# Storing paired-order output tiles with one transfer each in a fused retention and mixer kernel

## The chip, the cores and the metric

The kernel runs on one core of one Trainium2 chip. The metric is device time in microseconds (us) of one execution, the median of several runs. A run over 1.5% above the fastest of its kernel is called slow; ratios compare fast runs with fast runs. A profiled run adds a trace; the span of a profile is a little different from the timed median. Engines are named as follows: PE is TensorE's matmuls, PEld its weight loads, DVE is VectorE, ACT is ScalarE, POOL is GpSimd, SP is SyncE. A "q" after SP or ACT means the instruction queue of that engine, from which transfers are issued.

## The reference

```python
def reference(q, k, v, moe_U, moe_V, moe_w_ch1, moe_w_ch2):   # cut
    # q, k, v: (4, 8, 768, 64) float32: batch, heads, tokens, head dim
    state = 0
    for t in range(768):                      # retention, per head, decay gamma_h
        state = gamma * state + outer(k[:, :, t], v[:, :, t])
        y[:, :, t] = q[:, :, t] @ state / 8
    x = y as (4, 768, 512)
    u  = x + (x^T @ U @ V)^T                  # mixes the 768 tokens, rank 32
    return u + relu(u @ w_ch1) @ w_ch2        # 512 -> 2048 -> 512
```

The output is (4, 768, 512) float32: four batches of six tiles of 128 tokens, 256 KB a tile.

## The kernel before

The kernel works on the batches in a pipeline: while TensorE computes the MLP (`relu(u @ w_ch1) @ w_ch2`) of one batch, the retention of the next one is woven in. Tokens are held in pairs. Of a block of 128 tokens, partition 0 to 63 hold the even tokens and 64 to 127 the odd ones. So partition `64*two + p` is token `2*p + two`, and an output tile must be taken apart when it is stored:

```python
    HP = P // 2                       # 64
    stores = []

    def store():
        if stores:
            eng, dst, src = stores.pop(0)
            dst = dst.rearrange("(p two) c -> two p c", two=2)
            for i in range(2):
                eng.dma_start(out=dst[i], in_=src[ds(HP * i, HP)])
```

Each tile is two transfers of 64 partitions; each writes every second row of the block, in rows of 2 KB. Who issues them depends on the batch (batches count from 0):

```python
            # batch 0, after each tile's last sum:
                    stores.append((nc.scalar if b else nc.sync,
                                   out[b, ts(j, P)], o_sb))
            # batches 1 to 3:
            if end and i + 1 == NP:                    # last tiles of batch 3: half a tile
                stores.append((nc.sync, out[b, ts(j, P), ds(DQ * h, DQ)],
                               r[0][:, ds(DQ * h, DQ)]))
            elif r[1] == 2:
                stores.append((nc.sync if b > 1 else nc.scalar,
                               out[b, ts(j, P)], r[0]))
            # ... batch 3's last two tiles have more such pieces (quarters)
```

Batch 0's stores are kept until the end of its MLP (`weave(b == 1, ...)` keeps them) and then leave SyncE's queue all together. Batch 1's leave ScalarE's queue; those of batches 2 and 3 leave SyncE's as they are ready. SyncE's queue also carries every load and three kinds of DMA transposes, which read SBUF and write SBUF: `kT` and `qT` for the retention, and `uT`, the transposed input of the MLP, three for each of batches 2 and 3 (batches 0 and 1 get theirs in another way):

```python
    def lr_turn(b, j):                         # uT of two blocks of 128 tokens
        nc.sync.dma_start_transpose(
            out=uTs[b][:, ds(j, 2)].rearrange("p j c t -> p (j c) t"),
            in_=us[b][:, ds(j, 2)].rearrange("p j m -> p (j m)"))
```

The first two uT of a batch serve the first 512 tokens of its up-projection, and the third serves the other 256. The up-projection can't start without the first two, and not go past the eighth group of matmuls without the third.

## Time and profile before

| | before |
|---|---|
| median, at first | 226.73 us (3 runs, 225.97 to 227.8) |
| TensorE busy, of the 228.1 us span | 216.0 us (95%) |
| TensorE's longest wait | 1.8 us |
| store issues | 54 (40 from SP, 14 from ACT) |
| packets | 84,921 |

The head of the profile page (busy us, share of the span, number of instructions), and its DMA lines; each digit of the DMA line is the busy share, in tenths, of the 16 DMA engines in one fortieth of the span:

```profile
PE 216.0 (95%) x2235; PEld 148.4 (65%) x2235; DVE 140.8 (62%) x294; ACT 89.3 (39%) x187; POOL 91.8 (40%) x129
...
DMA  6997899999999999988999999000001990000263
...
DMA packets 84921, 38.83 MB, mean 170 GB/s; under 512 B 58816, under 2 KB 77984, under 8 KB 84896
```

TensorE is the bottleneck and is nearly always busy, so a transfer costs time only where TensorE waits for it, or at the very end. The waits view of TensorE (who waited for whom: total us, times, longest us) shows how little that is:

```profile
PE mlp L757 <- ACT gT L764: 1.8, 1, 1.8
...
PE mlp L757 <- DMA uT<-x: 0.5, 1, 0.5
```

The issue list of the page gives the stores' size and the median time from issue to landing:

```profile
out_dram<-o SPq DMA_DIRECT2D x32, 128.0 KB, 2.4
out_dram<-o ACTq DMA_DIRECT2D x12, 128.0 KB, 4.0
out_dram<-o SPq DMA_DIRECT2D x6, 64.0 KB, 2.1
```

The timeline of SyncE's queue (start us, us, engine and line, operation, times) shows where stores stand among other transfers:

```profile
94.87 7.59 SPq L608 DMA_DIRECT2D out_dram<-o  x12
102.51 1.33 SPq L155 DMA_DIRECT2D in<-in_k_dram  x2
...
174.44 3.71 SPq L608 DMA_DIRECT2D out_dram<-o  x6
178.32 3.87 SPq L591 DMA_TRANSPOSE uT<-x  x2
...
214.27 11.41 SPq L608 DMA_DIRECT2D out_dram<-o  x16
```

At 94.87 us batch 0's twelve halves go out just ahead of batch 3's 18 loads. At 174.44 batch 2's stand ahead of batch 3's uT transposes. From 214.27 to the end at 228.1 is the tail. Batch 1's stores leave ScalarE's queue between 123 and 138 us.

The stretches view (busy us of PE, PEld, DVE, ACT, POOL, then TensorE's granted clock, busy share of the DMA engines, GB/s) of batch 0's stores and of the tail:

```profile
97.50:105.50 8.00, 7.26 (x73) 4.42 (x71) 7.96 (x16) 4.70 (x12) 1.24 (x1) 1.00 0.91 205
...
214.30:228.10 13.80, 9.12 (x100) 8.20 (x97) 4.99 (x13) 0.00 (x0) 0.00 (x0) 0.91 0.49 114
```

Six tiles take 8 us at about 205 GB/s with the DMA engines nearly all busy (0.91). (The records of their packets run from 96.1 to 103.9 us; from 96 to 104 us the view reads 202 GB/s.)

### The profile page before, as it was taken

How to read it: one execution, taken by the hardware profiler on the slowest of the kernel's cores; microseconds unless marked ns; L12 is line 12 of the kernel's file. 1: busy time of each engine (PE TensorE's matmuls, PEld its weight loads, DVE VectorE, ACT ScalarE, POOL GpSimd, SP SyncE). 2: the span in 40 equal slices, each digit the busy share in tenths (PEclk: the TensorE clock that was granted, in tenths of full speed). 3: DMA queues.
4: the chain of work that ended last, by engine and by line, in shares of the span. 5: the costliest groups of instructions: out<-in, count | busy, mean ns of one | idle time of the engine just before them, and what ended most of it. 6: DMA issues, size and time to landing. Idle time of an engine off the chain costs nothing.

```text
span 228.1 us, 5543 instructions
## 1 busy us (share of the span) xinstructions
PE 216.0 (95%) x2235; PEld 148.4 (65%) x2235; DVE 140.8 (62%) x294; ACT 89.3 (39%) x187; POOL 91.8 (40%) x129
## 2 busy tenths in 40 slices
PE   7988999999899999989999996999999999999991
PEld 3677844595455454756887852656888846668891
DVE  6488556325274473899896653497868443857551
ACT  3256654474555126576411005567410035550000
POOL 5456777985879698930499400000000000000000
PEclk9999999999999999999999997999999999999997
DMA  6997899999999999988999999000001990000263
GB/s 177 299 290 211 239 367 288 367 357 228 239 181 240 242 228 180 192 205 210 237 236 229 215 252 193 1 0 3 0 3 42 154 204 17 3 1 0 48 148 83
DMA packets 84921, 38.83 MB, mean 170 GB/s; under 512 B 58816, under 2 KB 77984, under 8 KB 84896
## 3 DMA queue, kind: packets, MB, share of 16 engines
q1 hardware_dynamic: 83776, 36.84, 70.4%
q10 hardware_dynamic: 1120, 1.64, 2.4%
q8 instruction: 17, 0.28, 0.6%
q14 instruction: 8, 0.07, 0.1%
HBM read 27.46 MB, written 6.29 MB: 148 GB/s over the span
## 4 chain that ended last, share of the span: by engine, by line
PE 57%; DMA 17%; SPq 9%; DVE 8%; issue 3%; POOL 3%; ACT 1%; ACTq 0%; POOLq 0%; DVEq 0%
PE mlp L757 24%; PE A L649 9%; PE mlp L805 7%; DMA in<-in_moe_w_ch_dram 6%; SPq L155 5%; DMA in<-in_k_dram 4%; PE C L649 3%; DMA in<-in_q_dram 3%; SPq L591 3%; PE B L649 2%; DVE gS L599 2%; DMA qT<-qd 2%; PE s L505 2%; DVE a L511 2%; PE o L527 2%
## 5 line engine op out<-in xcount | busy, mean ns | idle before, releaser
L757 PE MATMUL mlp<-uT,w1b 128*128 128x512 f16 (+1 forms) x512 | 90.6, 330 | 2.5 <-ACT gT L764 1.8
L757 PEld LDWEIGHTS <-w1b 128*128 128x128 f16 x512 | 48.8, 99 | 34.9 <-issue 5.4
L764 ACT ACTIVATE gT<-mlp 128x512 f16<-128x512 f32 (+1 forms) x94 | 45.2, 491 | 66.0 <-PE mlp L757 30.8
L762 DVE TENSOR_SCALAR gT<-mlp 128x512 f16<-128x512 f32 (+1 forms) x34 | 18.9, 555 | 32.2 <-PE mlp L757 32.2
L511 DVE TENSOR_TENSOR a<-s,mask 128x512 bf16<-128x512 f32 x36 | 23.1, 682 | 12.6 <-PE s L505 12.4
L649 PEld LDWEIGHTS <-gT 128*128 128x128 f16 x288 | 27.5, 98 | 3.5
L805 PE MATMUL mlp<-w2b,gT 128*128 128x512 f16 x96 | 24.1, 380 | 0.0
L306 POOL TENSOR_TENSOR kd<-in,gk 128x512 bf16<-128x512 f32 x18 | 19.3, 1084 | 5.5 <-DMA in<-in_k_dram 5.5
L649 PEld LDWEIGHTS <-gS 128*128 128x128 f16 x200 | 19.3, 98 | 2.6
L85 ACT ACTIVATE x<-o 128x512 f16<-128x512 f32 x20 | 11.9, 595 | 21.5 <-PE o L527 21.3
L306 POOL TENSOR_TENSOR qd<-in,gq 128x512 bf16<-128x512 f32 x18 | 19.1, 1078 | 1.0 <-DMA in<-in_q_dram 1.0
L649 PE MATMUL A<-w2t,gT 128*128 128x256 f16 x144 | 18.3, 273 | 0.0
L85 ACT ACTIVATE state<-st 64x256 bf16<-64x256 f32 x40 | 15.0, 375 | 6.0 <-PE st L385 4.1
L805 PEld LDWEIGHTS <-gT 128*128 128x128 f16 x96 | 8.2, 98 | 7.5
L304 POOL CAST vd<-in 128x512 bf16<-128x512 f32 x18 | 11.2, 628 | 2.7 <-DMA in<-in_v_dram 2.2
L342 POOL CAST w1b<-in 128x512 f16<-128x512 f32 x16 | 9.7, 616 | 3.1 <-DMA in<-in_moe_w_ch_dram 2.7
L348 POOL CAST w2b<-in 128x512 f16<-128x512 f32 x16 | 9.7, 616 | 0.9 <-DMA in<-in_moe_w_ch_dram 0.2
L564 DVE TENSOR_TENSOR x<-s,x 128x256 f16<-128x256 f32 (+1 forms) x16 | 8.1, 550 | 2.1 <-ACT gT L764 1.1
L649 PE MATMUL B<-w2b,gT 128*128 128x256 f16 x72 | 9.4, 273 | 0.0
L649 PE MATMUL A<-w2t,gS 128*128 128x256 f16 x72 | 9.2, 273 | 0.0
L649 PE MATMUL A<-w2b,gT 128*128 128x256 f16 x72 | 9.0, 273 | 0.0
L527 PE MATMUL o<-vd,a 128*128 128x64 bf16 x144 | 7.7, 193 | 0.8 <-DVE a L511 0.8
(148 smaller groups left out, 278.4 us busy)
## 6 DMA issues: line engine op xcount, KB each, us to landing
in<-in_moe_w_ch_dram SPq DMA_DIRECT2D x32, 256.0 KB, 5.4
in<-in_k_dram SPq DMA_DIRECT2D x24, 256.0 KB, 5.3
in<-in_q_dram SPq DMA_DIRECT2D x24, 256.0 KB, 5.0
in<-in_v_dram SPq DMA_DIRECT2D x24, 256.0 KB, 5.4
out_dram<-o SPq DMA_DIRECT2D x32, 128.0 KB, 2.4
out_dram<-o ACTq DMA_DIRECT2D x12, 128.0 KB, 4.0
out_dram<-o SPq DMA_DIRECT2D x6, 64.0 KB, 2.1
Uf<-in_moe_U_dram SPq DMA_DIRECT2D x1, 96.0 KB, 5.8
```

The source lines that it names most:

```text
L85: nc.scalar.activation(dst, src, AF.Copy)
L155: nc.sync.dma_start(out=t, in_=src)
L304: nc.gpsimd.tensor_copy(out=t, in_=src)
L306: nc.gpsimd.tensor_tensor(t, src, g, op=ALU.mult)
L342: nc.gpsimd.tensor_copy(out=w1b[:, c, ts(mb, 512)], in_=take("w1", mb, c))
L511: nc.vector.tensor_tensor(a, four(sp[i]), causal(mask), op=ALU.mult)
L527: nc.tensor.matmul(o_p[:, ts(h, D)], a[i][:, h // 2], vb[:, h], start=(ci == 0 and h == 0), stop=True, skip_group_check=True)
L649: nc.tensor.matmul(acc[key, i], lhs[:, m, ts(i, P)], rhs[:, m], start=(fresh and m == 0), stop=(m == NH - 1), skip_group_check=True)
L757: nc.tensor.matmul(g_p[:, :sz], w1b[:, c, ts(m, P)], uTs[b][:, ds(j, nj), c], start=(c == 0), stop=(c == NCB - 1))
L762: nc.vector.tensor_relu(gT[:, m, ds(lo, sz)], g_p[:, :sz])
L764: nc.scalar.activation(gT[:, m, ds(lo, sz)], g_p[:, :sz], AF.Relu)
L805: nc.tensor.matmul(ch, gT[:, m, ts(j, P)], w2b[:, m], start=(m == 0), stop=(m == NM - 1))
```

## The change

The intent is half as many store issues, with transfers twice as large: the whole tile of 128 partitions goes in one transfer, and the pairs are taken apart by the access pattern of the DRAM side.

```diff
     def store():
         if stores:
             eng, dst, src = stores.pop(0)
-            dst = dst.rearrange("(p two) c -> two p c", two=2)
-            for i in range(2):
-                eng.dma_start(out=dst[i], in_=src[ds(HP * i, HP)])
+            eng.dma_start(out=dst.rearrange("(p two) c -> two p c", two=2),
+                          in_=src)
```

The SBUF side is 128 rows of 512 elements. The DRAM side is now a pattern of 2 x 64 x 512. Each row is still 2 KB, and the same bytes go to the same places. (Line numbers fall by one: a matmul of L757 before is L756 after.)

## The prediction

> **What bounds the kernel now.** TensorE is busy 216.0 of the 228.1 us span (the page's busy line) and holds 57% of the chain of waits; the waits view shows no TensorE wait over 1.8 us after 84 us. Stores matter in three places (the timeline). (a) From 95 us batch 0's six tiles leave SyncE's queue, just ahead of batch 3's 18 loads. (b) From 123 to 138 us batch 1's tiles leave ScalarE's queue, beside the transposes for batches 2 and 3. (c) From 174 us batch 2's tiles share SyncE's queue with batch 3's uT transposes (the chain shows uT 2.5 + 3.2 us, up to 184.1). Then the tail: first batch-3 store issued at 214.3, last at 225.1, end 228.1.
>
> **What the change removes.** 54 store issues become 27, each about 0.56 us of a queue: 15 us of issue, perhaps 1 us of it on the chain. Bytes and data packets (2 KB rows) stay.
>
> **What it adds.** The DRAM side becomes a 2 x 64 x 512 pattern, outermost dimension 2, not 64. [...] A 2 KB packet that met no traffic took 84 ns in the trace; 64 on one engine are 5.4 us for a 256 KB tile, about 7.4 us from issue to landing, against 2.4 us now. All tiles queue on the same two engines: six take 32 us (before: 8 us, 97 to 105 us).
>
> **Where that meets the critical path.** The program gives transfers eight completion semaphores in turn, so an issue also waits for the transfer eight before it, on either queue.
> 1. Batch 3's loads stand behind the stores on two engines: first landing about 132 instead of 107 us, last about 151. ScalarE's first batch-1 store waits for the 13th load (about 146), its last for an earlier store; ScalarE can't evacuate until 162 to 175 instead of 138. Batch 2's up-projection starts 24 to 36 us later, perhaps with a further stall for its third uT: estimate +33 us.
> 2. Batch 3's uT transposes stand behind three stores, then three more: +12 us to its start, +12 us before its second half: +24 us.
> 3. Tail: 1.5 MB through two engines is about 34 us (2 KB at 84, 1 KB at 45, 512 B at 27 ns); with latency 37 us after the first store instead of 13.8: +23 us.
>
> Sum: 226.7 + 33 + 24 + 23 = 307 us; I shade it to 303 us, range 262 to 332. Chances: faster by over 2% 0.04, within 2% 0.05, slower by over 2% 0.91.
>
> **What would show it.** The span to 95 us unchanged. Packets fall by about 810 (27 x 2 completion packets for 54 x 16), to some 84,110. Median store landing over 10 us. About 48 GB/s and 2/16 DMA share at the end, TensorE idle. TensorE waits near 138 and 184 us plus shifts. If stores still use 16 engines: packets fall by only 432, landings stay near 3 us, and time is within 1%.
>
> **What would make it wrong.** Engines chosen by the SBUF side's 128 (then same); loads overtaking stores; arbitration between the two queues kinder or harsher than packet by packet, which sizes step 1; a two-engine store faster than 84 ns per row.

## The result and the profile after

| | before | after |
|---|---|---|
| median of 4 runs | 226.75 us (225.97 to 227.8) | 318.1 us (317.39 to 318.59) |
| ratio of fast runs | | 1.402 (95% interval 1.396 to 1.409) |
| span of the profile | 228.1 us | 316.4 us |

A ratio is the mean time of one kernel's fast runs over that of the other's of the same rounds, so it is not quite the ratio of the medians. The change makes the kernel 40% slower, and the result is correct.

The head of the page and its DMA lines, after:

```profile
PE 220.5 (70%) x2235; PEld 150.4 (48%) x2235; DVE 140.7 (44%) x294; ACT 89.5 (28%) x187; POOL 91.1 (29%) x129
...
DMA  7999999999991122999999980000192910001111
...
DMA packets 84111, 38.82 MB, mean 123 GB/s; under 512 B 58006, under 2 KB 77174, under 8 KB 84086
```

The work is the same (DVE, ACT and POOL are busy as long as before), but the span grew by 88.3 us. Two things point at the cause. The packet count fell by exactly 810. In the trace of before a plain transfer ends with 16 packets of 4 bytes (called completion packets here); the nine stores of the tail after end with 2 each. 54 stores of 16 replaced by 27 stores of 2 is 864 - 54 = 810, and the 4-byte packets of the traces fell by just that, from 3,137 to 2,327. And the DMA line reads 1, about two sixteenths (a share of 0.12), at the end, where only stores run.

The waits view of TensorE, and the store lines of the tile view (duration of the issue in ns, min/median/max; first and last start):

```profile
PE mlp L756 <- DMA uT<-x: 66.5, 4, 34.0
...
L606 SPq DMA_DIRECT2D out_dram<-o x20: 512/2888/6394, 92.4 to 305.3; - x20
L606 ACTq DMA_DIRECT2D out_dram<-o x7: 522/533/4937, 140.4 to 290.2; - x7
```

TensorE waited 66.5 us for uT, against 0.5 before. Issuing a store held SyncE's queue for 2.9 us in the median and up to 6.4, against 0.57 (median) before. The issue list of this page has no landing times, for stores or loads, so the predicted landing can't be read there:

```profile
out_dram<-o SPq DMA_DIRECT2D x16, 256.0 KB
```

The timeline of SyncE's queue:

```profile
92.45 20.08 SPq L606 DMA_DIRECT2D out_dram<-o  x6
112.58 10.64 SPq L155 DMA_DIRECT2D in<-in_k_dram  x2
...
218.70 4.80 SPq L606 DMA_DIRECT2D out_dram<-o  x3
223.68 13.17 SPq L591 DMA_TRANSPOSE uT<-x  x2
...
281.08 27.57 SPq L606 DMA_DIRECT2D out_dram<-o  x8
```

The stretches of batch 0's stores, of a long wait of TensorE, of the first us after a wait, and of the tail:

```profile
95.00:127.00 32.00, 31.82 (x366) 24.70 (x365) 26.67 (x56) 11.72 (x26) 1.06 (x2) 1.00 0.20 66
146.00:162.00 16.00, 0.00 (x0) 0.00 (x0) 0.00 (x0) 0.00 (x0) 0.61 (x1) 0.50 0.96 77
187.20:192.50 5.30, 5.28 (x36) 3.70 (x37) 1.97 (x6) 1.70 (x5) 0.00 (x0) 0.62 0.00 0
...
281.10:316.40 35.30, 9.14 (x100) 8.22 (x97) 4.99 (x13) 0.00 (x0) 0.00 (x0) 0.68 0.12 45
```

Batch 0's six tiles now take 32 us instead of 8, while TensorE is still busy. In the tail the DMA engines are at a share of 0.12, that is 2 of 16, and move 45 GB/s. TensorE ends its work in the first 9 us of it and the stores go on for 26 more. From 146 to 162 us TensorE does nothing, at a granted clock of 0.50, while the DMA engines are nearly all busy (0.96) and yet move only 77 GB/s; an experiment below comes back to that.

Three marks of the timelines of SyncE's queue divide the loss. They are the first store of batch 0, of batch 2 and of batch 3:

| stretch | before | after | longer by | predicted |
|---|---|---|---|---|
| start to first batch-0 store | 94.87 | 92.45 | -2.4 | 0 |
| to first batch-2 store | 79.57 | 126.25 | 46.7 | 33 |
| to first batch-3 store | 39.83 | 62.38 | 22.6 | 24 |
| to the end | 13.8 | 35.3 | 21.5 | 23 |
| sum (spans) | 228.1 | 316.4 | 88.3 | 80 |

Most of the third line (19.6 of 22.6 us) is two waits of TensorE, for the uT pair of batch 3 and for its third uT, in the changed kernel's timeline (in brackets: idle time before it, and what ended it):

```profile
238.91 8.81 PE L756 MATMUL mlp<-uT,w1b 128*128 128x512 f16 x32 [11.09 <-DMA uT<-x]
256.18 4.08 PE L756 MATMUL mlp<-uT,w1b 128*128 128x256 f16 x21 [8.46 <-DMA uT<-x]
```

The first line is the scatter of single runs: in the other profiles, in which nothing differs up to this mark, it lies between 90.7 and 95.2 us.

### The profile page after: what moved, and what is told of

Its sections match the earlier page's. It is cut to its first block, busy times and chain, and to the rows that moved or that the text cites. A ratio compares the mean times of both kernels' runs of the same rounds, so it can differ in the third digit from the quotient of the medians.

```text
span 316.4 us, 5507 instructions
## 1 busy us (share of the span) xinstructions
PE 220.5 (70%) x2235; PEld 150.4 (48%) x2235; DVE 140.7 (44%) x294; ACT 89.5 (28%) x187; POOL 91.1 (29%) x129
## 2 busy tenths in 40 slices
DMA packets 84111, 38.82 MB, mean 123 GB/s; under 512 B 58006, under 2 KB 77174, under 8 KB 84086
## 4 chain that ended last, share of the span: by engine, by line
PE 40%; DMA 25%; SPq 17%; DVE 5%; POOL 2%; issue 2%; ACT 1%; POOLq 0%; DVEq 0%
PE mlp L756 15%; DMA uT<-x 10%; SPq L155 7%; PE A L648 6%; DMA in<-in_v_dram 6%; SPq L591 5%; DMA in<-in_moe_w_ch_dram 5%; PE mlp L804 5%; SPq L474 4%; DMA in<-in_k_dram 4%; PE C L648 2%; PE mlp L189 2%; PE B L648 2%; DVE gS L599 1%; PE s L505 1%
## 5 line engine op out<-in xcount | busy, mean ns | idle before, releaser
L756 PE MATMUL mlp<-uT,w1b 128*128 128x512 f16 (+1 forms) x512 | 95.4, 342 | 66.6 <-DMA uT<-x 66.5
L756 PEld LDWEIGHTS <-w1b 128*128 128x128 f16 x512 | 50.6, 102 | 102.0 <-DMA uT<-x 67.5
L87 DVE COPY qO<-qT 128x512 bf16<-128x512 bf16 x12 | 3.9, 366 | 30.4 <-DMA qT<-qd 30.4
```

What stands on the lines that cost most here:

```text
L756: nc.tensor.matmul(g_p[:, :sz], w1b[:, c, ts(m, P)], uTs[b][:, ds(j, nj), c], start=(c == 0), stop=(c == NCB - 1))
```

## The experiments

The theory: the outermost dimension of the DRAM side, 2, puts each store on two DMA engines (2 completion packets a store, a DMA share of 0.12 in the tail). All stores then form one line on these two, by estimate 5.4 us a tile (64 rows of 84 ns). Loads and transposes, it assumes, have a share on each of 16 engines, the two among them (a load ends with 16 completion packets in the trace, which names no engine), so they wait for that line too; and TensorE waits for the transposes.

Rival 1: fewer issues shift the turn of the eight completion semaphores (101 and 103 to 109 in the traces, one an issue), and so the waits. Rival 2: a strided store from all 128 partitions is slow in itself. Rival 3, which the prediction itself held for a part of the loss: ScalarE is held by its own stores and can't evacuate for TensorE.

The kernels of the first table below give wrong rows on purpose.

### More rows in the outermost dimension: 16, 8 and 4

```diff
-            eng.dma_start(out=dst.rearrange("(p two) c -> two p c", two=2),
+            eng.dma_start(out=dst.rearrange("(p n) c -> n p c", n=16),   # 8, 4
                           in_=src)
```

One transfer a tile, the same bytes in rows of 2 KB, the same issues and semaphores; only the outermost dimension (and which row goes where, wrongly) differs from the changed kernel.

> The changed kernel with 16 in place of 2 as the outermost dimension of the DRAM pattern (rows go to the wrong places on purpose; one transfer a tile, the same rows of 2 KB, the same issues and semaphores). Theory (the outermost dimension sets how many engines carry a store): sixteen engines, 84,111 + 27 x 14 = 84,489 packets, store landing near 3 us, 225 to 229 us. Rival 1 (fewer issues shift the turn of the eight semaphores and so the waits): about 318 us, since issues and semaphores are those of the changed kernel. Rival 2 (a strided store from all 128 partitions is slow in itself): about 318 us.

> As n16 with 8 (wrong rows on purpose). Theory: eight engines, a tile takes 16 x 84 ns = 1.3 us on each, six tiles about 8 us as the halves of before; packets 84,273; 225 to 233 us. Rivals 1 and 2: about 318 us.

> As n16 with 4 (wrong rows on purpose). Theory: four engines, a tile takes 32 x 84 ns = 2.7 us on each, six tiles 16 us; packets 84,165; tail +6, batch 3's uT +6, loads and batch 1's stores +8: 238 to 255 us. Rivals 1 and 2: about 318 us.

| outermost dimension | median us | before, same job | ratio of fast runs | packets | 2 KB rows per us, batch 0's stores |
|---|---|---|---|---|---|
| 2 (the change) | 318.1 | 226.75 | 1.402 | 84,111 | 23.9 |
| 4 | 264.57 (4 runs) | 227.89 | 1.170 (1.154 to 1.187) | 84,165 | 42.7 |
| 8 | 236.65 (4 runs, 1 fast: 231.62) | 227.89 | none given | 84,273 | 67.7 |
| 16 | 224.25 (6 runs) | 227.89 | 0.994 (0.984 to 1.005) | 84,489 | 119.6 |
| 64 twice (before) | | | | 84,921 | 98.1 |

The last column counts the records of 2 KB packets in the traces, from the first to the last of batch 0's. All four packet counts are exactly those of n completion packets a store. With 16 the whole loss is gone, though issues, semaphores, row size and the 128 partitions are those of the changed kernel. So rivals 1 and 2 fall. (Seven of the eleven runs before in this job are slow; the median of the four fast ones is 225.8 us, and the ratios use these. The record classes 4 as "unclear", as it does two runs below, though all three intervals lie above 1.1; the reason isn't on record.)

The dose fits in direction, but the rate doesn't grow in step with n: with 8 the six tiles took 11.3 us instead of the 8 expected. The size with 4 was expected too small (238 to 255, measured 264.57): TensorE waited 29.6 us for uT in that run, the same kind of wait that the prediction undersized. With 8 only one run counts as fast (231.62, inside the expected range); the others, 236 to 239 us, don't, and how much 8 costs is not settled.

The stretch of batch 0's stores with 16, to be read against the 205 GB/s of before (their packets run from 92.0 to 98.5 us, where the view reads 264):

```profile
93.30:99.70 6.40, 6.07 (x58) 3.78 (x58) 6.26 (x14) 4.02 (x9) 1.29 (x2) 1.00 1.02 270
```

The stores themselves do gain from one transfer of 128 partitions, when it ends with 16 completion packets: about 265 GB/s, in one profile of each kernel, with other rows written than before. In batch 0's stretch a 2 KB packet of a 64-partition half took 152 ns in the median (mean 142), one of these stores 84 ns (mean 117); why is not shown. The kernel's gain, 0.6%, is not clear of noise; the waits view of before shows no TensorE wait for stores that could be won.

### The change for some batches only

```diff
     def store():
         if stores:
-            eng, dst, src = stores.pop(0)
+            eng, dst, src, one = stores.pop(0)
+            if one:                       # b == 0, 1, 2, 3, or b < 2
+                eng.dma_start(out=dst.rearrange("(p two) c -> two p c", two=2),
+                              in_=src)
+                return
             dst = dst.rearrange("(p two) c -> two p c", two=2)
             ...
```

> The change for batches 0 and 1 only, the halves of before for batches 2 and 3 (right result). Theory: the first term alone; the first batch-2 store comes 44 to 48 us later than before, as in the changed kernel, and nothing is added after it: 226.7 + 46 = 270 to 277 us. The prediction had 33 us for this term (260). Rival: stages interact (the late stores need the early ones' backlog), so the sum of the parts falls well short of the whole: under 265 us here.

> The change for batch 0 only. Theory: batch 3's loads stand behind 32 us of stores on two engines, and ScalarE's first batch-1 store waits for the 13th of them; but batch 1's stores do not share the two engines row by row with the transposes: batch 2's up-projection starts 12 to 18 us later, no long second wait for uT: 237 to 247 us. If the queue sharing does not matter, this alone gives nearly all of the first term: about 270 us.

> The change for batch 1 only. Theory: 384 store rows a queue on two engines from about 124 us, turn by turn with the transposes' 256-byte packets (102 ns instead of 18 for one of them): batch 2's first uT pair about 12 us later and its third about 10 us more: 240 to 256 us. If the queues did not share the engines packet by packet: under 235 us.

> The change for batch 2 only. Theory: batch 3's uT transposes behind three stores, then three more: +20 to +24 us, 246 to 252 us; store rows before the transposes in the same queue, transposes' packets at 18 ns, not 102.

> The change for batch 3 only. Theory: the tail alone: first batch-3 store to the end about 35 us instead of 13.8: 246 to 250 us, everything before it unchanged within 2 us.

| changed batches | median us | before, same job | longer by | ratio of fast runs |
|---|---|---|---|---|
| 0 | 247.9 | 227.24 | 20.7 | 1.090 (1.082 to 1.099) |
| 1 | 252.2 | 227.24 | 25.0 | 1.113 (1.107 to 1.120) |
| 0 and 1 | 275.05 | 227.89 | 47.2 | 1.223 (1.211 to 1.234) |
| 2 | 252.13 | 227.24 | 24.9 | 1.112 (1.103 to 1.122) |
| 3 | 248.9 | 227.24 | 21.7 | 1.097 (1.091 to 1.103) |
| all | 318.1 | 226.75 | 91.4 | 1.402 |

All results are correct. The medians are of all runs, slow ones too. By medians of fast runs alone the differences are 19.7, 25.1, 49.2, 25.0, 21.8 and 91.4 us. The parts add up: 19.7 + 25.1 + 25.0 + 21.8 = 91.6 against 91.4 us, where each ratio's interval is about 2 us to either side. So each batch's stores cost by themselves, in their own place. Batch 2 alone came out just above what was expected (252.13 against 246 to 252); the others lie inside by their fast runs (batch 0: 246.8).

Batch 0's cost was expected as a start of batch 2's up-projection 12 to 18 us later. In its profile (of a slow run) TensorE has one long wait for uT, 21.7 us, so this size was missed. There the stores' packets had ended at 128.6 us. SyncE's queue, held by them, issued batch 3's loads from 115.3 to 143.9 us (before: 102.5 to 121.3) and the first uT behind these only at 148.9. So here the transposes are late because they are issued late, and not because their packets stand in a line.

The timeline of TensorE shows where batch 1's 25.0 us come from (brackets as above):

```profile
148.19 4.36 PE L761 MATMUL mlp<-uT,w1b 128*128 128x512 f16 x12 [16.35 <-DMA uT<-x]
...
166.11 2.74 PE L761 MATMUL mlp<-uT,w1b 128*128 128x256 f16 x12 [8.13 <-DMA uT<-x]
```

Two waits, one for the uT pair and one for the third uT: 24.5 us together. The changed kernel has the same two, longer, since batch 0's stores delay the loads and so the transposes too:

```profile
164.32 4.23 PE L756 MATMUL mlp<-uT,w1b 128*128 128x512 f16 x12 [33.97 <-DMA uT<-x]
...
187.22 2.74 PE L756 MATMUL mlp<-uT,w1b 128*128 128x256 f16 x12 [12.99 <-DMA uT<-x]
```

34.0 + 13.0 = 47.0 us, which is the 46.7 us of that stretch.

### Batch 1's stores from SyncE's queue

In the changed kernel ScalarE's queue is held by its six stores from 140.4 to 168.9 us. Rival 3 says that this is what TensorE waits for. The kernel with the change for batch 1 only was run again with those stores issued by SyncE:

```diff
             elif r[1] == 2:
-                stores.append((nc.sync if b > 1 else nc.scalar,
+                stores.append((nc.sync,
                                out[b, ts(j, P)], r[0], b == 1))
```

> As the kernel with the change for batch 1 only, but batch 1's stores leave SyncE's queue, so ScalarE's queue is never held by a store. Theory (the transposes for batch 2 wait for the two engines; which queue the stores stand in only sets whether they wait behind the stores or turn by turn with them): uT pair behind three stores, about +13 us, third uT behind three more, about +15 us: 246 to 262 us, the transposes' 256-byte packets back at 18 ns. Rival (ScalarE, held from 140 to 169 us in the changed kernel by its own stores and so unable to evacuate, is what costs; this was a step of the prediction): under 235 us.

Measured: 253.63 us (4 runs; before 226.61), ratio 1.121 (1.112 to 1.129), correct. So nothing was won by freeing ScalarE in this kernel. The test isn't a clean one, since the same move puts the stores ahead of the transposes in SyncE's queue. The timeline of TensorE has the two waits again, divided otherwise:

```profile
144.73 4.24 PE L761 MATMUL mlp<-uT,w1b 128*128 128x512 f16 x12 [13.02 <-DMA uT<-x]
...
166.95 2.74 PE L761 MATMUL mlp<-uT,w1b 128*128 128x256 f16 x12 [12.54 <-DMA uT<-x]
```

In the changed kernel rival 3 does not fall. In the trace of before TensorE ran four groups of four matmuls of the up-projection and then waited for ScalarE to evacuate the first ones (`gT<-mlp`). ScalarE's first evacuations and TensorE's matmuls, before and then after:

```profile
138.13 1.57 ACT L764 ACTIVATE gT<-mlp 128x512 f16<-128x512 f32 x3 [17.82 <-DVE gT L762]
...
138.78 1.02 PE L757 MATMUL mlp<-uT,w1b 128*128 128x512 f16 x4 [1.79 <-ACT gT L764]
```

```profile
168.62 2.13 PE L756 MATMUL mlp<-uT,w1b 128*128 128x512 f16 x8
169.07 1.57 ACT L763 ACTIVATE gT<-mlp 128x512 f16<-128x512 f32 x3 [51.60 <-PE st L489]
```

After the change TensorE's fifth group (the second four of these eight) began at 169.72 us, and the first of ScalarE's three evacuations had ended at 169.67. The uT pair had ended the long wait at 164.3, but with uT in time the fifth group would still have waited for ScalarE. The two holds end together there (and 0.8 us apart in the kernel that changes batch 0 only), and no run took away only one of them in the changed kernel.

The records of single packets tell how the transposes were held (10th, 50th and 90th percentile, ns):

| kernel | stretch, us | 256 B packets (transposes) | 2 KB packets (stores) |
|---|---|---|---|
| change for batch 1, ACT queue | 130 to 146 | 18, 105, 184 | 84, 84, 84 |
| the same, SP queue | 128 to 142 | 18, 18, 62 | 84, 84, 84 |
| the same, SP queue, no stores running | 142.2 to 147.7 | 18, 18, 25 | none |

From two queues, the times fit turns of one or two rows: about half of the 256 B packets take 60 to 120 ns, near their own 18 plus one store row's 84, and a third take 160 to 190, near 18 plus two rows. The stores slow down a little too: 20.6 rows per us for all of batch 1's against 23.9 for the first three from SyncE's queue. From one queue, the transposes stand behind whole stores and then run at 18 ns. The sum comes out nearly the same; that this is because the two engines have the same rows to move either way is argued, not shown.

A stretch view of each, first from ScalarE's queue, then from SyncE's:

```profile
130.00:148.00 18.00, 1.85 (x23) 1.32 (x21) 3.01 (x9) 0.00 (x0) 0.00 (x0) 0.62 1.35 86
```

```profile
128.00:144.00 16.00, 3.71 (x40) 2.99 (x38) 3.85 (x11) 0.00 (x0) 0.00 (x0) 0.69 0.77 79
```

In the first, the DMA engines read as fully busy (1.35, so the records of packets overlap) at only 86 GB/s. So the stretched packets are hardly those of the two engines alone that carry stores: at 105 ns each, one after the other, two engines could by estimate move some 300 packets of 256 B in 16 us, and the trace has 2,698 from 130 to 146 us. By this estimate the transposes slow down on far more engines than these two; the trace kept does not name a packet's engine, so that is not shown directly, and why stays open.

### The tail of before from two queues

The tail remained as a place to gain. The kernel before was run with the second half of each of batch 3's stores issued from ScalarE's queue, idle by then (`b_now` is set before each batch's `weave`):

```diff
             for i in range(2):
-                eng.dma_start(out=dst[i], in_=src[ds(HP * i, HP)])
+                (nc.scalar if i and b_now[0] == 3 else eng).dma_start(
+                    out=dst[i], in_=src[ds(HP * i, HP)])
```

> The kernel before (two halves of 64 rows a tile), with the second half of each of batch 3's stores issued from ScalarE's queue, which is free by then. If the tail of before is limited by the issue time on SyncE's queue (16 issues in 11.4 us, the last at 225.1 us, 1.3 us after the last arithmetic): 0.5 to 1.2 us faster than before, 225.6 to 226.3 us. If it is limited by the last data and the landing: the same within 0.3 us.

Measured: 226.56 us (6 runs) against 226.61 (11 runs), ratio 1.002 (0.996 to 1.008). In the profiles the tail is as long as before (13.9 against 13.8 us from the first store to the end). So no gain from a second queue was seen, though the interval leaves room for up to 0.8 us. This version doesn't beat the kernel before.

## Why the prediction was right or wrong

**That stores would go to two engines: right.** The trace of before does not show it; in the prediction it was the author's estimate. The traces of the runs fit it for outermost dimensions of 2, 4, 8 and 16: as many completion packets a store (the packet counts agree to the last packet), and 23.9, 42.7, 67.7 and 119.6 rows per us. Two engines at 84 ns a row would pass 23.8.

**What a store costs there: right.** 64 rows of 84 ns on each engine were predicted as 5.4 us a tile and 32 us for six. Batch 0's took 32.1 us, and the median 2 KB packet 84 ns. The loads behind them came about 5 us earlier than predicted: GpSimd took up the first at 127.3 us (predicted 132) and the 13th at 140.4 (146). The last landed at 152.7 (the chain of waits), near the predicted 151, but by luck: the loads' data packets had started by 142.7 us, and this landing came 12.2 us after its issue, beside batch 1's stores, which the prediction had not counted there.

**The tail: right.** +23 us predicted, +21.5 in the traces and +21.7 in the kernel that changes batch 3 only.

**Batch 3's uT: right.** +24 us predicted, as a wait for the pair and one for the third (measured waits 11.1 and 8.5 us): +22.6 in the traces, +24.9 in the kernel that changes batch 2 only.

**The first term, batches 0 and 1: right in kind, too small.** The prediction put: "Batch 2's up-projection starts 24 to 36 us later, perhaps with a further stall for its third uT: estimate +33 us." The first wait alone is 34.0 us. The further stall, which the estimate left unpriced, is 13.0 us. The term measured +46.7 us, and +47 to +49 in the kernel that changes these two batches only. This is most of the 15 us between the predicted 303 and the measured 318.1.

**Who holds TensorE there: right, but only half of it.** The prediction's step "ScalarE can't evacuate until 162 to 175" came true (held until 168.9). The trace puts the first wait down to uT (until 164.3), but ScalarE would have held TensorE to the same point (the fifth group at 169.7 us, 138.8 before). So the first wait has two causes that end together; by this trace, freeing one alone would not have won it, but no run shows that. In the kernel that changes batch 1 only, the loss stayed with ScalarE free (253.63 against 252.2 us). The second wait, until 187.2, was for the third uT.

**What was not in the sum.** After each long wait TensorE's clock was low for a while: mean 0.62 in the 5.3 us after 187.2 us, then 1.00. The up-projection's matmuls took 342 ns in the mean instead of 330, 4.8 us of busy time in all. In the trace the granted clock went to 0.50 in each of the four waits for uT, 2.9 to 5.0 us after it began, and was 1.00 again from 191.2 us, 4.0 us after the work began; after the three other waits it took 3.0 to 3.5 us. How much of these 4.8 us lies on the critical path was not tested.

**What was to be removed.** 27 issues of 0.57 us did go away. They weren't on the critical path: the kernel with 16 outermost rows saves the same issues and is at most 1.6% faster by the interval, perhaps not at all. The saved queue time turned into more: the remaining issues held SyncE's queue 2.9 us each in the median and up to 6.4, against 0.54 in the median in the kernel with 16 outermost rows.

**What stays open.** A correct one-transfer store with 16 outermost rows would need the tile in another token order. The run with 16 puts its gain near 0.6%, not clear of noise, and it was not built. How much the store with 8 outermost rows costs is not settled either. Nor is the share of uT and of ScalarE in the first wait of the changed kernel, nor why the transposes slow down on far more engines than two, as the estimate above has it.

## What to carry to other kernels

Before two transfers are merged into one, write down the outermost dimension of both access patterns as the instruction will carry them: here, with 128 partitions on the SBUF side throughout, 2, 4, 8 and 16 on the DRAM side gave as many completion packets a store, and 23.9, 42.7, 67.7 and 119.6 rows per us. To read it off a trace, count completion packets per transfer (2 here, 16 before), or look for a DMA share of a few sixteenths at a stretch that should be busy (0.12 in the tail here). And price a slow transfer by what queues on the same engines, not by its own bytes: here stores that nobody waits for cost 70 of 91 us through the loads and transposes behind them and the engine queue that they hold.
